# Single-bank PSUM tiles, folds on VectorE, natural query order and a pinned instruction order in a fused attention and gate kernel

## The chip, the cores and the metric

The kernel runs on one core of a Trainium2 chip. The metric is the device time of one execution in microseconds, and its median is quoted. The core has a matrix engine (PE, with its weight loads as PEld), VectorE (DVE), ScalarE (ACT), GpSimd (POOL) and SyncE (SP), which run side by side and wait for one another through semaphores. PE writes its results to a memory called PSUM; the changed program divides what it uses of it into eight tiles of 2 KB a partition, here called banks. DVE and ACT read them there; no instruction of POOL does in these kernels. The profile is of one execution; its span is about 2 us shorter than that execution's time.

Executions of the kernel before fell between 545 and 551 us or between 552 and 556 us. A run counts as slow when it is over 1.5% above the fastest of its set. The set of the main result has two runs of the kernel before, both of the longer kind, so both count as fast. The profile of the kernel before is of a 545.95 us execution.

## The reference

```python
# b, h = 8, 8   s = 576   d = 64   f = 128
def phi(x):                                   # x: [b, h, s, d]
    proj = x @ w_phi                          # d -> f
    proj = proj - max(abs(proj), axis=-1)     # per row
    return concat([exp(proj), exp(-proj)])    # 2 f features
q_p, k_p = phi(q), phi(k)
kv  = einsum('bhsf,bhsd->bhfd', k_p, v)
z   = k_p.sum(axis=2)
x   = (q_p @ kv) / (q_p @ z + 1e-6)           # attention, heads joined: [8, 576, 512]

x1, x2, x3 = split(x @ w_proj, 3)             # 512 -> 3 x 512
x2_conv = irfft(rfft(x2, axis=1) * rfft(filter, axis=0))
out = (x1 * x2_conv * x3) @ w_out
```

The symbol `@` is a matrix product. The kernel does the attention in 16 units (half the heads of a batch each) and the gate in 8, one a batch. The Fourier transforms are matmuls with sine tables. A *fold* makes the sums and differences of rows n and 576 - n in front of the forward transform.

## The kernel before

Every piece of work is a `Step` with a nominal time for each engine. A planner orders the steps from three streams: loads, then attention, then gate as filler where attention would make the PE wait. A scheduler may still move instructions, taking emission order as priority.

```python
def proj(c, shape, name):                     # double-bank tiles, two of them
    return c.psum.tile(shape, FP32, name=name, tag="proj", bufs=2)
def b1(c, shape, dtype, name):                # single-bank tiles, four
    return c.psum.tile(shape, dtype, name=name, tag="b1", bufs=4)
...
def fold(c, eng, x, GG, k0, nk, name):
    ...
    xs = x[:, k0:k0 + nk, 0:289]
    xr = x[:, k0:k0 + nk, 576:287:-1]         # read backwards
    eng.tensor_tensor(out=eo[:, :, 0, :], in0=xs, in1=xr, op=ALU.add)
    eng.tensor_tensor(out=eo[:, :, 1, :], in0=xs, in1=xr, op=ALU.subtract)
    ...                                       # two more on eo, and a small copy
...
def main(dst, src, g0, g1):                   # loads of k, q, v: partition p takes
    nc.gpsimd.dma_start(                      # rows 4p..4p+3
        out=dst[:, g0:g1].rearrange("p g h c d -> p (g h) (c d)"),
        in_=src[b, 4 * g0:4 * g1, 0:512, :].rearrange("h (p c) d -> p h (c d)", c=4))
...
def pq_a(hp):
    pp = proj(c, [P, 2, 4, P], "Pq")
    for j in range(2):
        ...                                   # two matmuls, q^T x w_phi
    for j in range(2):                        # row order restored by a strided write
        nc.scalar.activation(s.Eqp[hp][:, j].rearrange("f (p c) -> f c p", c=4),
                             pp[:, j], AF.Exp, bias=0.0, scale=1.0)
def pq_b(hp):                                 # adds -2 max, then the same with scale=-1.0
    ...
def fld():
    fold(c, nc.gpsimd, xTs[b], c.G[b % 2], kt, 2, "x")
...
for st in pl.run([loads, attn, gate], (1, 26, 12).__getitem__):
    st.fn()
```

Here `Eqp` and `Eqm` are the positive and negative exponentials of the query projection `Pq`; `Ekp` and `Ekm` are those of the key projection `Pk`.

## Time and profile before

| before | |
|---|---|
| time | 554.18 us, median of 2 (552.48 to 555.89) |
| profiled span, granted PE clock | 544.2 us, 0.918 |
| PE, DVE, ACT, POOL busy | 399.0, 307.6, 346.1, 262.8 us |
| both exponentials of Pq | 128 of 1374 and 1356 ns |
| a gate with nothing beside it | 25.7 us |

The busy table and the slices of the page of the kernel before; in the slices each digit is the busy share in tenths of a fortieth of the span, and PEclk is the clock granted to the PE:

```profile
## 1 busy us (share of the span) xinstructions
PE 399.0 (73%) x3680; PEld 247.1 (45%) x3725; DVE 307.6 (57%) x575; ACT 346.1 (64%) x604; POOL 262.8 (48%) x352
...
PE   2346673767778276775666786888689899999996
...
DVE  6991493338658332952653773777356556554453
ACT  3999634897995278568659749783984460515150
POOL 9749999198327932841592151553153343400000
PEclk9996695779898877989978999999899999999999
```

No engine is full, and the PE's digits rise to 9 only at the end. The stage windows show the two regimes; columns are the window, its length, busy us with instruction counts of PE, PEld, DVE, ACT and POOL, then clock, DMA share and GB/s:

```profile
core 0: us, PE busy (x) PEld busy (x) DVE busy (x) ACT busy (x) POOL busy (x), PEclk, DMA share, GB/s
...
200.00:240.00 40.00, 28.89 (x332) 19.84 (x334) 23.41 (x43) 26.83 (x47) 23.32 (x33) 0.87 0.40 46
...
440.00:480.00 40.00, 39.69 (x271) 20.19 (x276) 25.17 (x39) 15.92 (x30) 18.36 (x18) 1.00 0.11 34
```

From 200 to 240 us the PE is busy 28.9 of 40 us beside attention; from 440 it is busy 39.7 with gates and, until 455 us, the last transposes of attention (the last folds run on POOL), while ACT and DVE have room. A gate then takes 25.7 us (like ACT copies at 485.4 and 511.1 us in the timeline). What the first regime waits for is in the chain of work that ended last, first its shares of the whole span:

```profile
PE 32%; ACT 32%; POOL 19%; issue 6%; DVE 5%; DMA 4%; POOLq 0%; DVEq 0%; ACTq 0%
```

Then a stretch of the same chain, in the order of time (start, us, what):

```profile
207.68 2.45 ACT Eqp L696 x2
...
210.80 0.87 ACT Eqm L708
211.85 1.40 ACT Eqp L696
213.25 1.14 ACT Eqm L708
214.38 1.13 ACT Eqp L696
...
216.39 1.20 ACT Eqm L708
```

The groups of instructions (engine, operation, out<-in, count; busy us, mean ns; idle before and its releaser) give the price of those exponentials and, for comparison, that of Pk:

```profile
L708 ACT ACTIVATE Eqm<-Pq 128x512 bf16<-128x512 f32 x64 | 85.1, 1356 | 9.4 <-PE Pq L705 8.7 <-PE KV L724 0.5
L696 ACT ACTIVATE Eqp<-Pq 128x512 bf16<-128x512 f32 x64 | 81.2, 1374 | 41.2 <-PE Pq L690 41.0
...
L601 ACT ACTIVATE Ekp<-Pk 128x512 bf16<-128x512 f32 x64 | 40.3, 629 | 27.0 <-DVE mxk L598 26.9
```

Both read 128x512 fp32 and write 128x512 bf16. The only difference is the output's step, 8 bytes against 2, and the time doubles.

### The profile page before, as it was taken

To read this page: it belongs to the slowest core of one execution; us is meant where nothing else is said; L and a number is where in the kernel's file an instruction comes from. 1 tells how busy PE (TensorE), PEld (TensorE's weight loads), DVE (VectorE), ACT (ScalarE), POOL (GpSimd) and SP (SyncE) were. 2 spreads that over 40 slices of the span, in tenths; PEclk is the share of its full clock that TensorE was granted. 3 is DMA by queue.
4 is the path that set the end of the run, shared out by engine and by line. 5 is a ranking of instruction groups with operands and counts; after the bars stand their busy time and mean duration, and the time that the engine had idled before them with its cause. 6 is when DMAs were issued, how large, how long until landed. Compare 5 with 4: busy or idle time off the path is not lost.

```text
span 544.2 us, 9323 instructions
## 1 busy us (share of the span) xinstructions
PE 399.0 (73%) x3680; PEld 247.1 (45%) x3725; DVE 307.6 (57%) x575; ACT 346.1 (64%) x604; POOL 262.8 (48%) x352
## 2 busy tenths in 40 slices
PE   2346673767778276775666786888689899999996
PEld 2234562444445253553443464545445545454443
DVE  6991493338658332952653773777356556554453
ACT  3999634897995278568659749783984460515150
POOL 9749999198327932841592151553153343400000
PEclk9996695779898877989978999999899999999999
DMA  6993494047009103704533000200020020211202
GB/s 69 150 201 44 46 130 45 12 52 81 2 2 124 7 3 38 90 16 87 77 43 43 0 2 13 75 1 2 1 88 0 3 87 1 89 46 42 78 12 87
DMA packets 45707, 27.04 MB, mean 50 GB/s; under 512 B 14752, under 2 KB 40544, under 8 KB 45664
## 3 DMA queue, kind: packets, MB, share of 16 engines
q0 software_dynamic: 40256, 16.88, 26.0%
q1 hardware_dynamic: 5408, 9.57, 5.2%
q8 instruction: 29, 0.48, 0.3%
q14 instruction: 14, 0.11, 0.1%
HBM read 33.75 MB, written 9.44 MB: 79 GB/s over the span
## 4 chain that ended last, share of the span: by engine, by line
PE 32%; ACT 32%; POOL 19%; issue 6%; DVE 5%; DMA 4%; POOLq 0%; DVEq 0%; ACTq 0%
ACT Eqp L696 12%; ACT Eqm L708 11%; PE acc L928 9%; PE acc L969 6%; PE acc L893 3%; DMA ks<-in_k_dram 3%; PE acc L995 3%; ACT Ekp L601 2%; ACT Ekm L602 2%; PE Pq L705 2%; PE NE L744 2%; ACT CS L903 1%; POOL eox L365 1%; DVE mxk L598 1%; DMA out_dram<-o 1%
## 5 line engine op out<-in xcount | busy, mean ns | idle before, releaser
L696 ACT ACTIVATE Eqp<-Pq 128x512 bf16<-128x512 f32 x64 | 81.2, 1374 | 41.2 <-PE Pq L690 41.0
L708 ACT ACTIVATE Eqm<-Pq 128x512 bf16<-128x512 f32 x64 | 85.1, 1356 | 9.4 <-PE Pq L705 8.7
L928 PE MATMUL acc<-xT,wproj 128*128 128x64 bf16 (+1 forms) x501 | 66.6, 286 | 1.1 <-ACT x1s L938 0.5
L705 PE MATMUL Pq<-mT,sel 128*128 128x512 bf16 x64 | 28.4, 443 | 50.6 <-ACT Eqp L696 33.6
L598 DVE TENSOR_REDUCE mxk<-Pk 128x4 f32<-128x512 f32 x64 | 43.7, 685 | 30.5 <-PE Pk L589 26.4
L601 ACT ACTIVATE Ekp<-Pk 128x512 bf16<-128x512 f32 x64 | 40.3, 629 | 27.0 <-DVE mxk L598 26.9
L895 ACT CAST x2n<-acc 128x512 bf16<-128x512 f32 x40 | 24.1, 617 | 44.4 <-PE acc L893 21.3
L928 PEld LDWEIGHTS <-wproj 128*128 128x128 bf16 x512 | 34.0, 98 | 35.2 <-issue 6.3
L969 PE MATMUL acc<-IV,Y 128*128 128x512 bf16 (+1 forms) x255 | 40.0, 292 | 0.5
L602 ACT ACTIVATE Ekm<-Pk 128x512 bf16<-128x512 f32 x64 | 39.2, 613 | 0.0
L589 PE MATMUL Pk<-wpp,kT 128*128 128x256 bf16 x128 | 22.9, 312 | 13.2 <-DVE mxq_244 L624 6.1
L1001 DVE COPY o<-acc 128x512 f32<-128x512 f32 (+1 forms) x24 | 16.5, 687 | 28.2 <-PE acc L995 19.5
L728 ACT CAST KVs<-KV 128x260 bf16<-128x260 f32 x32 | 14.1, 443 | 28.8 <-PE KV L724 28.8
L748 DVE RECIPROCAL rc<-NE 128x10 f32<-128x10 f32 x32 | 6.9, 218 | 44.2 <-PE NE L744 44.1
L721 PEld LDWEIGHTS <-Ekp 128*128 128x128 bf16 x256 | 16.1, 106 | 31.7 <-issue 24.3
L744 PE MATMUL NE<-KVs,Eqp 128*128 128x65 bf16 x256 | 24.7, 199 | 7.5 <-ACT Eqm L708 6.7
L624 DVE TENSOR_REDUCE mxq_251<-Qn 128x8 f32<-128x1024 f32 x16 | 19.5, 1221 | 18.7 <-PE Qn L621 18.0
L621 PE MATMUL Qn<-wpp,qT 128*128 128x256 bf16 x128 | 21.4, 296 | 11.6 <-ACT Ekm L602 5.0
L953 DVE TENSOR_TENSOR ts<-acc,x1s 128x512 bf16<-128x512 f32 x32 | 21.9, 690 | 10.6 <-PE acc L928 10.4
L749 DVE TENSOR_TENSOR xn<-NE,rc 128x640 bf16<-128x640 f32 x32 | 26.2, 821 | 0.8
L969 PEld LDWEIGHTS <-Y 128*128 128x128 bf16 x256 | 18.9, 101 | 16.3 <-issue 2.0
L744 PEld LDWEIGHTS <-Eqm 128*128 128x128 bf16 x256 | 19.9, 101 | 13.4 <-issue 11.5
(468 smaller groups left out, 1179.7 us busy)
## 6 DMA issues: line engine op xcount, KB each, us to landing
out_dram<-o SPq DMA_DIRECT2D x32, 256.0 KB, 2.0
ks<-in_k_dram POOLq DMA_DIRECT2D x7, 512.0 KB, 6.1
qs<-in_q_dram POOLq DMA_DIRECT2D x7, 512.0 KB, 8.0
vs<-in_v_dram POOLq DMA_DIRECT2D x7, 512.0 KB, 6.0
wproj<-in_moe_w_proj_dram POOLq DMA_DIRECT2D x4, 384.0 KB, 11.3
out_dram<-o SPq DMA_DIRECT2D x8, 128.0 KB, 2.3
ks<-in_k_dram POOLq DMA_DIRECT2D x2, 256.0 KB, 4.4
qs<-in_q_dram POOLq DMA_DIRECT2D x2, 256.0 KB, 4.5
```

What stands on the lines that cost most here:

```text
L589: nc.tensor.matmul(pp[:, j, 2 * cp:2 * cp + 2, :], lhsT=s.kT[:, hp + 2 * j, cp, :], rhs=c.wpp, start=True, stop=True)
L598: nc.vector.tensor_reduce(out=mx[:, 4 * i:4 * i + 4], in_=pp[:, i], axis=AX.X, op=ALU.max, apply_absolute_value=True)
L601: nc.scalar.activation(Ep[:, j], pp[:, j], AF.Exp, bias=0.0, scale=1.0)
L602: nc.scalar.activation(Em[:, j], pp[:, j], AF.Exp, bias=0.0, scale=-1.0)
L696: nc.scalar.activation(s.Eqp[hp][:, j].rearrange("f (p c) -> f c p", c=4), pp[:, j], AF.Exp, bias=0.0, scale=1.0)
L705: nc.tensor.matmul(pp[:, j], lhsT=c.sel[:, 2 * hp + j, :], rhs=s.mT[:, 0:512], start=False, stop=True, skip_group_check=True)
L708: nc.scalar.activation(s.Eqm[hp][:, j].rearrange("f (p c) -> f c p", c=4), pp[:, j], AF.Exp, bias=0.0, scale=-1.0)
L744: nc.tensor.matmul(av[:, j, ci, :], lhsT=E, rhs=s.KVs[hp][:, j, sg, :], start=(sg == 0), stop=(sg == 1))
L749: nc.vector.tensor_tensor(out=s.xn[:, :, hp, :, :], in0=av[:, :, :, 0:HD].rearrange("p j c d -> p c j d"), in1=rc.rearrange("p j c o -> p ...
L895: nc.scalar.copy(x2n[:, m, :], acc)
L928: nc.tensor.matmul(acc, lhsT=c.wproj[:, kt, base + m * P:base + (m + 1) * P], rhs=xTs[b][:, kt, s0:s1], start=(kt == 0), stop=(kt == 3))
L969: nc.tensor.matmul(acc, lhsT=Y, rhs=c.IV[:, kt, s0:s1], start=(i == 0), stop=(i == 5))
```

## The change

Its intent: relieve ACT of the strided writes and POOL of the folds, let each PSUM bank go as soon as its own half is read, and start gates early, in an order worked out beforehand and pinned on each engine. Cut to its core (the order table, the split reductions and the smaller moves are cut):

```diff
-def proj(c, shape, name):
-    return c.psum.tile(shape, FP32, name=name, tag="proj", bufs=2)
 def b1(c, shape, dtype, name):
-    return c.psum.tile(shape, dtype, name=name, tag="b1", bufs=4)
+    return c.psum.tile(shape, dtype, name=name, tag="b1", bufs=8)
...
-            main(s.qs, q, g0, g1)
+            for ci in range(4):               # 256-byte packets in place of 1024
+                nc.gpsimd.dma_start(
+                    out=stage("qs")[:, g0:g1, :, ci].rearrange("p g h d -> p (g h) d"),
+                    in_=q[b, 4 * g0:4 * g1, ci * P:(ci + 1) * P, :].rearrange("h p d -> p h d"))
...
-            pp = proj(c, [P, 2, 4, P], "Pq")
+            pp = [b1(c, [P, 4, P], FP32, "Pq") for j in range(2)]   # also Pk, Qn, NE
-                    s.Eqp[hp][:, j].rearrange("f (p c) -> f c p", c=4), pp[:, j],
+                nc.scalar.activation(s.Eqp[hp][:, j], pp[j].rearrange("f c p -> f (c p)"),
...
-        fold(c, nc.gpsimd, xTs[b], c.G[b % 2], kt, 2, "x")          # and the filter's folds
+        fold(c, nc.vector, xTs[b], c.G[b % 2], kt, 2, "x")
...
-            if ci % 2:
-                nc.scalar.copy(o[0:rows, :], acc[0:rows, :])
-            else:
-                nc.vector.tensor_copy(o[0:rows, :], acc[0:rows, :])
+            nc.scalar.copy(o[0:rows, :], acc[0:rows, :])
...
-    for st in pl.run([loads, attn, gate], (1, 26, 12).__getitem__):
-        st.fn()
+    pl, order = make_plan(...)      # each step has a wanted time from a table; the planner takes
+                                    # the step with the least (lateness + weight * wanted time)
+    with tc.manual_schedule(engines={PE, Activation, DVE, Pool}):   # emission order is kept
+        for st in order:
+            st.fn()
```

## The prediction

> **What bounds the kernel now.** The profiled span is 544.2 us and no engine is full: PE 73%, ACT 64%, DVE 57%, POOL 48% (busy table). To about 440 us attention and gate overlap, PE busy 22 to 36 of every 40 us (stage windows). After that only gate work is left: PE busy 39.5 of 40, 25.7 us a batch (like ACT copies at 485.4 and 511.1 us in the timeline). Before that the chain of waits runs through ACT: the exponentials of Pq are 22% of the span (all ACT 32%), POOL 19%; PE waits 33.6 and 16.4 us for those exponentials (waits). They cost 1374 and 1356 ns; those of Pk, of the same shape and types, 629 and 613. Only the output step differs (8 bytes against 2); the trace agrees with the Trainium skill, "SBUF — State Buffer", the note on cachelines: full rate needs at least two hits in a 16-byte line.
>
> **What changes.**
> - Natural q order makes those 128 writes contiguous: about -95 us of ACT. 24 output copies come from DVE: +15. ACT 346 -> 266 us.
> - Folds leave POOL: 16 x about 5.3 us and two filter folds, -99 us. q loads become four DMAs each: 27 more issues at 0.9 us. POOL 263 -> 185.
> - Folds on DVE: 18 of four tensor_tensors and small copies. Contiguous bf16 ones of 1024 and 512 elements take 0.69 and 0.42 us here, so 0.45 for 578 in that mode, 0.75 outside it. The Trainium skill, "Vector Engine (DVE) Microarchitecture Reference", section 5.1, leaves a negative step unmeasured; one input of each reads backwards. I expect 2.2 to 3.3 us a fold: +50. Output copies -16.5, split reductions +5, split normalisation +11, memsets +3. DVE 308 -> 360: the fullest engine.
> - Eight single banks replace two double and four single slots: a bank is free after its own half.
> - The fixed order spreads the gate: the first starts once four attention units have begun, the last attention transpose is at 81% of the matmuls' time (changed instruction order).
>
> **Sum.** PE work is unchanged: 752,640 moving columns, of which a gate has 59,392; at the tail's 25.7 us per gate that is 326 us at full clock (estimate), 350 at a granted 0.93. DVE needs 360. Per batch: PE 44, DVE 41, ACT 30 us. Overlap will not be perfect: I take 48 to 49 us a batch, 388 for eight, plus 35 us of start (sine tables, DVE 35 busy of the first 40 us, unchanged) and 5 of drain. Predicted: 428 us, range 398 to 468, 8 in 10. About 90 of the 126 us are ACT time on the chain; the rest is the merged tail and POOL. Chances: faster by over 2% 0.96, within 2% 0.02, slower 0.02.
>
> **What would show it.** Right: exponentials of Pq near 0.62 us; PE busy above 7 tenths in nearly every slice after the first three; a chain of PE and DVE, almost no POOL; DVE above 80%; clock up from 0.918. Wrong: exponentials above 1 us; fold operations above 0.8 us or stretched beside POOL (before, the gate's products stretched from 0.69 to 1.68 us); a new wait for q loads, whose packets shrink from 1024 to 256 bytes.
>
> **What would make it wrong.** A fixed order from nominal times stalls all engines where real times differ (exponential 0.48 nominal, 0.6 here): then 460 or more. Folds at 0.45 us an operation: 400 or less.

## The result

The changed kernel takes 435.79 us (434.49 and 437.09) against 554.18. The ratio of the fast runs is 0.7864, 95% interval 0.7719 to 0.8008. A ratio here is the mean time of one kernel's fast runs over that of the other's of the same rounds, so it is not quite the ratio of the quoted medians. The forecast was 428, in a range of 398 to 468. The two runs of the kernel before in this set are of the longer kind; against its fast runs in the sets below (means 548 to 550 us) the gain is about 113 us and not 118, a ratio of about 0.79.

The same parts of the page, after:

```profile
## 1 busy us (share of the span) xinstructions
PE 363.8 (84%) x3725; PEld 230.3 (53%) x3725; DVE 339.9 (78%) x758; ACT 272.9 (63%) x628; POOL 183.2 (42%) x236
...
PE   1311778669997999888999988999999999999995
...
DVE  5994679965995899649999799989998889552741
ACT  1886736089665874568748965399647887354322
POOL 9964805670186326626473294329431241000000
PEclk9999988699998999999999998999999999999999
```

From the tenth slice on the digits of the PE are 9 or 8 but for one 7 and the last; its first four are lower than before. The windows that answer to those shown, and the first:

```profile
core 0: us, PE busy (x) PEld busy (x) DVE busy (x) ACT busy (x) POOL busy (x), PEclk, DMA share, GB/s
0.00:40.00 40.00, 7.71 (x46) 5.29 (x46) 28.61 (x86) 26.16 (x44) 30.31 (x50) 1.00 1.04 129
...
200.00:240.00 40.00, 37.22 (x439) 24.79 (x438) 38.83 (x84) 27.87 (x70) 23.40 (x28) 1.00 0.58 73
...
360.00:400.00 40.00, 39.11 (x337) 20.97 (x335) 23.87 (x50) 21.15 (x41) 0.32 (x1) 1.00 0.09 31
```

From 200 to 240 us the PE does gate and attention together, 37.2 us busy, and DVE is busy 38.8 of 40. The chain has gone over to these two, over the whole span:

```profile
DVE 43%; PE 37%; ACT 9%; POOL 4%; issue 3%; DMA 3%; ACTq 0%; POOLq 0%
```

and in the same stretch as before, from about 200 us:

```profile
211.32 1.20 DVE mxk L595 x2
212.51 1.79 DVE ts L946 x3
214.31 1.20 DVE mxq_247 L621 x2
...
216.68 1.28 DVE mxq_247 L621 x2
217.95 1.19 DVE mxk L595 x2
...
220.77 0.60 DVE yT_262 L972
```

The groups, in the order of those above, and the first two operations of a fold, now on DVE:

```profile
L598 ACT ACTIVATE Ekp<-Pk 128x512 bf16<-128x512 f32 x64 | 39.2, 612 | 59.7 <-PE Pk L586 41.3 <-DVE mxk L595 18.1
...
L704 ACT ACTIVATE Eqm<-Pq 128x512 bf16<-128x512 f32 x64 | 36.3, 663 | 3.1 <-PE Pq L699 3.1
L691 ACT ACTIVATE Eqp<-Pq 128x512 bf16<-128x512 f32 x64 | 34.9, 629 | 1.2 <-PE Pq L685 1.1
...
L363 DVE TENSOR_TENSOR eox<-xT 128x578 bf16<-128x578 bf16 x16 | 9.8, 610 | 0.6
...
L364 DVE TENSOR_TENSOR eox<-xT 128x578 bf16<-128x578 bf16 x16 | 7.7, 479 | 0.0
```

The exponentials of Pq now cost what those of Pk cost.

### The profile page after: what moved, and what is told of

The parts are those of the page before. It is cut to its first block, busy times and chain, and to the rows that moved or that the text cites. A ratio compares the mean times of both kernels' runs of the same rounds, so it can differ in the third digit from the quotient of the medians.

```text
span 435.2 us, 9441 instructions
## 1 busy us (share of the span) xinstructions
PE 363.8 (84%) x3725; PEld 230.3 (53%) x3725; DVE 339.9 (78%) x758; ACT 272.9 (63%) x628; POOL 183.2 (42%) x236
## 4 chain that ended last, share of the span: by engine, by line
DVE 43%; PE 37%; ACT 9%; POOL 4%; issue 3%; DMA 3%; ACTq 0%; POOLq 0%
PE acc L962 5%; DVE mxk L595 5%; PE acc L921 5%; PE acc L886 5%; PE acc L988 5%; DVE xn L743 4%; DMA out_dram<-o 3%; DVE mxq_247 L621 3%; DVE ts L946 3%; DVE mxq_254 L621 2%; PE KV L716 2%; DVE xT L766 2%; PE Pq L685 2%; PE NE L738 2%; PE Pq L699 1%
## 5 line engine op out<-in xcount | busy, mean ns | idle before, releaser
L921 PE MATMUL acc<-xT,wproj 128*128 128x512 bf16 (+1 forms) x512 | 72.5, 288 | 0.0
L962 PE MATMUL acc<-IV,Y 128*128 128x512 bf16 (+1 forms) x256 | 38.9, 286 | 0.0
L704 ACT ACTIVATE Eqm<-Pq 128x512 bf16<-128x512 f32 x64 | 36.3, 663 | 3.1 <-PE Pq L699 3.1
L991 ACT COPY o<-acc 128x512 f32<-128x512 f32 (+1 forms) x40 | 23.5, 601 | 21.0 <-PE acc L988 12.5
L691 ACT ACTIVATE Eqp<-Pq 128x512 bf16<-128x512 f32 x64 | 34.9, 629 | 1.2 <-PE Pq L685 1.1
L511 POOL DMA_DIRECT2D qs<-in_q_dram x36 | 31.3, 906 | 5.0 <-DMA wproj<-in_moe_w_proj_dram 3.9
L743 DVE TENSOR_TENSOR xn<-NE,rc 128x320 bf16<-128x320 f32 x64 | 31.4, 491 | 2.2
L896 ACT CAST CS<-acc 128x512 bf16<-128x512 f32 x40 | 23.1, 622 | 13.7 <-PE acc L378 11.1
L738 PE MATMUL NE<-KVs,Eqm 128*128 128x65 bf16 x256 | 22.7, 196 | 0.0
L738 PEld LDWEIGHTS <-Eqp 128*128 128x128 bf16 x256 | 19.6, 99 | 3.0 <-DVE kT L562 0.4
L621 DVE TENSOR_REDUCE mxq_254<-Qn 128x4 f32<-128x512 f32 x32 | 20.0, 682 | 0.7 <-PE Qn L618 0.6
```

The lines of the kernel that those rows point to most:

```text
L511: nc.gpsimd.dma_start(out=stage("qs")[:, g0:g1, :, ci].rearrange("p g h d -> p (g h) d"), in_=q[b, 4 * g0:4 * g1, ci * P:(ci + 1) * P, :]. ...
L621: nc.vector.tensor_reduce(out=mxq[:, 0:4, 2 * hp + j], in_=pp, axis=AX.X, op=ALU.max, apply_absolute_value=True)
L691: nc.scalar.activation(s.Eqp[hp][:, j], pp[j].rearrange("f c p -> f (c p)"), AF.Exp, bias=0.0, scale=1.0)
L704: nc.scalar.activation(s.Eqm[hp][:, j], pp[j].rearrange("f c p -> f (c p)"), AF.Exp, bias=0.0, scale=-1.0)
L738: nc.tensor.matmul(av[:, ci, :], lhsT=E, rhs=s.KVs[hp][:, j, sg, :], start=(sg == 0), stop=(sg == 1))
L743: nc.vector.tensor_tensor(out=s.xn[:, :, hp, j, :], in0=av[:, :, 0:HD], in1=rc.to_broadcast([P, 5, HD]), op=ALU.mult)
```

## The experiments

Each kernel was run four times (three rounds and a profile) beside the kernel before, whose median over all its runs, slow ones included, lay between 553.6 and 554.8 us in every set. The ratios use its fast runs (mean 548 to 550 us), and so do the gains given here. The sets ran on different chips, so a difference of a few us between kernels of different sets is uncertain. All gave correct results. The changed kernel itself was not run again in these sets, so it enters with its 435.8 us from its own set. "Pinned" is the fixed order on every engine.

### e1: natural query order alone, in the kernel before

```diff
-            main(s.qs, q, g0, g1)
+            (the four DMAs of the change)
-                    s.Eqp[hp][:, j].rearrange("f (p c) -> f c p", c=4), pp[:, j],
+                    s.Eqp[hp][:, j], pp[:, j].rearrange("f c p -> f (c p)"),     # Eqm alike
```

> The kernel before with one part of the change: natural q order (four q DMAs a load, contiguous exponentials of Pq). Theory A (the ACT time on the chain is most of the gain): exponentials of Pq fall to about 0.62 us, ACT busy from 346 to about 255 us, time about 490 us (0.88 of before); the gate-only tail of about 100 us stays, which is why it is not 440. Rival B (the merged order is the gain, ACT was only one of several equal chains): 530 us or more, the chain moving to POOL.

Measured: 501.28 us (500.54 to 502.65), ratio 0.9118 (0.9044 to 0.9192). ACT fell to 264.5 us busy and the exponentials to 616 and 621 ns, about as forecast. The gain is 49 us against the fast runs, from 82 us less ACT work. ACT falls from 32% of the chain to 10%, and the shares are now these:

```profile
PE 44%; POOL 25%; DVE 10%; ACT 10%; issue 6%; DMA 5%; POOLq 0%; DVEq 0%; ACTq 0%
```

The windows at the end of the same profile:

```profile
core 0: us, PE busy (x) PEld busy (x) DVE busy (x) ACT busy (x) POOL busy (x), PEclk, DMA share, GB/s
400.00:440.00 40.00, 40.00 (x277) 20.15 (x276) 26.80 (x41) 13.61 (x26) 15.74 (x16) 1.00 0.09 31
440.00:480.00 40.00, 40.00 (x257) 19.42 (x255) 19.21 (x33) 16.55 (x31) 0.00 (x0) 1.00 0.18 60
```

POOL is now a quarter of the chain (19% before), and at the end there are again 80 us and more in which the PE is full, DVE is a third to a half idle and ACT more than half. Theory A comes nearer (about 490 forecast); rival B's 530 was missed, but it is right that other chains stood close behind ACT.

### e2: the strided writes put back into the changed kernel

```diff
-            (the four DMAs of the change)
+            main(stage("qs"), q, g0, g1)
-                nc.scalar.activation(s.Eqp[hp][:, j], pp[j].rearrange("f c p -> f (c p)"),
+                nc.scalar.activation(s.Eqp[hp][:, j].rearrange("f (p c) -> f c p", c=4), pp[j],   # Eqm alike
```

> The changed kernel with one part undone: q loaded and exponentials written in the old order (8-byte output step), everything else and the instruction order kept. Theory A: ACT busy rises by 90 us to about 365, ACT becomes the fullest engine, time about 475 us (1.09 of the changed kernel). Rival B: ACT had 37% idle, the order hides most of it, below 450 us.

Measured: 495.95 us (495.49 to 496.07), ratio to before 0.9017 (0.8946 to 0.9088), 60 us more than the changed kernel. ACT is busy 354.2 us and is 38% of the chain. It is the fullest engine after the PE, but with 72% not a full one; the loss is larger than either theory said. It may be that in the pinned order every late exponential also delays what stands behind it; that is argued, not shown.

### e3: the folds back on POOL

```diff
-        fold(c, nc.vector, xTs[b], c.G[b % 2], kt, 2, "x")
+        fold(c, nc.gpsimd, xTs[b], c.G[b % 2], kt, 2, "x")     # and the filter's, and the border copy
```

> The changed kernel with the folds back on POOL, order kept. Theory A: DVE drops by 40 us to about 300, POOL rises to about 283 us; a fold takes 5.3 us in place of 2.3 and v products wait behind it, time 455 to 470 us, POOL on the chain again. Rival B: DVE was the fullest engine (37 to 39 of 40 us busy between 200 and 320 us), so its relief wins and the time is 430 us or less.

Measured: 449.45 us (449.40 to 450.00), ratio 0.8173 (0.8094 to 0.8251), 14 us slower than the changed kernel. POOL rose to 286.4 us busy and is 12% of the chain. DVE fell to 310.4, by 29.5 us and not by the 50 that the folds had taken: part of it went into the gate's products on DVE, whose groups rose from 32.4 to 40.9 and from 11.1 to 16.6 us. The trace shows them slowed beside the folds on POOL: of the 48 products of 1024 elements in those groups, the 18 with no POOL instruction beside them took 0.68 to 0.69 us, and all 12 that took 1.17 to 1.77 us ran beside a fold operation. The folds' move is worth 14 us although it loads the engine that is now the fullest after the PE: nearer to theory A, but below its 455 to 470 us.

### e8: the order rule of before, pinned

```diff
-        (make_plan's table)
+        return pl, pl.run_streams([loads, attn, gate], (1, 26, 12).__getitem__)
```

> The changed kernel with the order rule of the kernel before (three streams, attention first, gate filling in), still fixed on each engine; all else of the change kept. Theory A: a gate-only tail of about 100 us comes back, in which DVE and ACT are under half busy, and their work is squeezed into the rest: 465 to 480 us. Rival B: the order is worth little once ACT is relieved: below 445 us.

Measured: 478.18 us (475.09 to 481.31), ratio 0.8696 (0.8612 to 0.8779), 42 us slower than the changed kernel. The windows from 360 us show the gates alone again:

```profile
core 0: us, PE busy (x) PEld busy (x) DVE busy (x) ACT busy (x) POOL busy (x), PEclk, DMA share, GB/s
360.00:400.00 40.00, 40.00 (x373) 22.57 (x372) 25.63 (x62) 15.79 (x30) 0.00 (x0) 1.00 0.12 43
400.00:440.00 40.00, 40.00 (x263) 19.50 (x262) 20.71 (x39) 19.49 (x36) 0.00 (x0) 1.00 0.14 48
```

PE full, DVE 20.7 to 25.6 and ACT 15.8 to 19.5 of 40. In the changed kernel DVE's work is spread, and only the last 75 us look like that. This is theory A. The Trainium skill ("Perfetto Trace Analysis", Optimization Strategy) says that where the most-contended engine changes over time, interleaving those regimes may help; here it is worth 42 us.

### e4 and e5: the pinning alone

```diff
-    with tc.manual_schedule(engines={...}):
-        for st in order:
-            st.fn()
+    for st in order:                       # e4: the changed kernel, free
+        st.fn()
```

e5 does the reverse: the loop of the kernel before is put into `manual_schedule`.

> The changed kernel without the fixed order per engine: the instructions are emitted in the same order, but the scheduler may move them. Theory A (what counts is the merged emission order, the pinning little): 437 to 450 us. Rival B (the pinning itself carries the order's 42 us): 470 us or more.

> The kernel before, with its own emission order pinned on each engine, nothing else. Theory A: pinning alone is worth little, ratio 0.97 to 1.03 (538 to 570 us). Rival B: pinning is a good part of the gain, below 525 us.

Measured: e4 420.56 us (419.79 to 421.72), ratio 0.7681 (0.7637 to 0.7724); e5 640.18 us (638.07 to 641.18), ratio 1.1684 (1.1613 to 1.1754). Both misses: pinning is not worth little, it costs. It costs 92 us in the kernel before (against its fast runs) and 15 us in the changed one. e4 is the fastest kernel. Of DVE's waits this one changes most (us in total, times, longest us), here pinned:

```profile
DVE mxk L595 <- ACT Ekm L599: 17.0, 13, 5.7
```

and here free:

```profile
DVE mxk L595 <- ACT Ekm L599: 5.4, 8, 2.4
```

The maxima of Pk, kept in their place, stand 17.0 us behind exponentials of ACT; free, 5.4 us. That these waits make up the 15 us is not shown. DVE leads the chain no more: PE 53%, DVE 33%, in place of DVE 43% and PE 37%. The order of emission still counts when it isn't pinned, as e10 shows.

### e13: only the PE pinned

```diff
-    with tc.manual_schedule(engines={PE, Activation, DVE, Pool}):
+    with tc.manual_schedule(engines={PE}):
```

> The changed kernel with only the PE pinned to the planned order; ACT, DVE and POOL are left to the scheduler. It asks where the 15 us between the changed kernel (436) and the unpinned one (421) lie. Theory A (the planned order of DVE and ACT, made from durations that are too short for them, is what stalls; the PE order is good): 419 to 426 us. Rival B (the PE order holds up the others): 432 to 438 us.

Measured: 425.85 us (425.35 to 426.05); no ratio was given, as only one of the seven runs of the kernel before in this set counted as fast (545.91 us; the others 554.45 to 555.44). Of the 15 us, about 10 come back when DVE, ACT and POOL are free, and about 5 lie in the PE's order (about 1%, between different sets, so uncertain). Theory A, with a share for the PE. That the short nominal times are the reason fits the numbers (0.48 us nominal for a 512-element exponential, 0.61 to 0.66 measured; 0.60 for a 512-element reduction, 0.68 measured), but no plan with corrected times was run, so the reason was only argued.

### e6 and e9: double-bank tiles, pinned and free

```diff
-    return c.psum.tile(shape, dtype, name=name, tag="b1", bufs=8)
+    return c.psum.tile(shape, dtype, name=name, tag="b1", bufs=4)
+def pair2(c, name):
+    t = c.psum.tile([P, 2, 4, P], FP32, name=name, tag="proj", bufs=2)
+    return [t[:, 0], t[:, 1]]
-            pp = [b1(c, [P, 4, P], FP32, "Pq") for j in range(2)]
+            pp = pair2(c, "Pq")                                   # Pk, Qn and NE alike
```

> The changed kernel with the memory of before for matmul results: two double-bank tiles for Pk, Qn, Pq and the normaliser, four single-bank ones for the rest; the order, made for eight single banks, is kept. Theory A: a pair is free only when both halves are read, so the matmuls in front of DVE reductions and ACT exponentials wait longer: 450 to 470 us, new waits of Pk, Qn and NE matmuls for DVE and ACT. Rival B: banks were never short, 440 us or less.

> The changed kernel with two double-bank and four single-bank tiles (as e6) and without the pinned order (as e4). Theory A (most of the 154 us of e6 are an order made for eight banks that cannot move; the banks themselves are worth less): 440 to 470 us, 20 to 50 over the 421 of e4. Rival B (single banks are the largest part of the change whatever the order): 520 us or more. Rival C (worth nothing): within 8 us of e4.

Measured: e6 589.50 us (586.18 to 592.45), ratio 1.0762 (1.0673 to 1.0850), slower than the kernel before. e9 464.0 to 465.2 us in its three fast runs, ratio 0.8462 (0.8358 to 0.8566). e6 is 154 us over the changed kernel, far past theory A; e9 is 44 us over e4, as its theory A said. So the single banks are worth some 44 us, and another 110 us of e6 is an order that was made for eight banks and could not move. The order of emission of e9 was still the one made for eight banks, so part of the 44 us may be the order's; that was not tested. The new waits of the PE in e6, longest first (us in total, times, longest us):

```profile
PE NE L746 <- DVE xn L751: 49.0, 32, 3.4
PE Qn L624 <- DVE mxq L627: 33.1, 32, 5.3
```

In the changed kernel neither wait is among the PE's ten longest.

One execution of e9, the profiled one, took 965.72 us and is left out. It is described in the last section.

### e10: the order rule of before, free

> The changed kernel with the order rule of before (as e8) and without pinning (as e4). Theory A (the merged order of emission is worth its 42 us also to a scheduler that may move things, since it works by emission order): 455 to 475 us. Rival B (the scheduler recovers the merging by itself): 430 us or less.

Its edit is that of e8 and that of e4 together. Measured: 452.87 us (449.87 to 454.84), ratio 0.8239 (0.8116 to 0.8362). That is 32 us over e4 and 25 under e8. The result lies between the theories and close to A: the merged order is worth 32 us even to a scheduler that may move instructions.

### e7: output copies back on DVE

```diff
-            nc.scalar.copy(o[0:rows, :], acc[0:rows, :])
+            (nc.vector.tensor_copy for even ci, as before)
```

> The changed kernel with 24 of the 40 output copies back on DVE: DVE plus 16 us (about 356), ACT minus 15. Theory A (DVE is nearly full from 200 to 320 us, so it is the limit there): 5 to 12 us slower, 441 to 448 us. Rival B (PE and waits limit it): within 3 us of the changed kernel.

Measured: 439.70 us (438.65 to 440.17), ratio 0.8022 (0.7968 to 0.8076). DVE's busy time rose by 13.6 us and the time by 4 us, a little under theory A. The difference is about 1%, between kernels of different sets, so the size is uncertain.

### e12: an attempt at something faster

The six tables of the inverse transform are made just before the first gate needs them, in tiles of their own, without pinning.

```diff
-    for g in trig_groups(c):
+    trig = trig_groups(c)
+    for g in trig[:4]:
         g()
...
     for st in order:
+        if st.name == "m0.x10":
+            for g in trig[4:]:             # POOL writes the counter again for each
+                g()
         st.fn()
```

> An attempt at something faster: e4 with the six sine tables of the inverse transform made just before gate 0 needs them and not in the first 40 us (their DVE work of about 10 us and their table loads leave the start; an integer counter is written by POOL each time). Theory A (DVE work is the chain of the first 60 us): 8 to 12 us off e4, 408 to 413 us. Rival B (the same work is only moved to where DVE is nearly full as well): 418 us or more.

Measured: 431.33 us (431.28 to 433.27), ratio 0.7864 (0.7786 to 0.7943), 11 us slower than e4. A failure, as rival B expected. The start did get faster: the PE was busy 19.0 of the first 40 us, against 13.5 in e4. The loss came where the tables went (65.7 to 121.0 us in the trace): from 100 to 120 us the PE was busy 12.3 of 20 us, against 19.4 in e4. Its new waits are for the products of v on POOL (7.4 us), which the counters may have delayed; that was not tested.

## Why the prediction was right

The time was 8 us above the forecast and well inside the range. Point by point:

- **Strided writes: right in mechanism, too large on the chain.** 1374 and 1356 ns became 629 and 663. ACT was forecast at 266 us and measured 272.9. But "about 90 of the 126 us are ACT time on the chain" was too much: natural order alone gave 49 us (e1), and its removal from the changed kernel cost 60 (e2). The other terms are larger than "the rest".
- **Merged regimes: right, and larger than I made it.** 42 us pinned (e8), 32 us free (e10).
- **Single banks: not sized in the prediction.** 44 us when the instructions may move (e9). They are not a detail.
- **Folds: right in size, with one of its own signs of error in part.** Each of the four operations was expected at 0.45 to 0.75 us and measured a mean of 0.48 to 0.61; but 11 of the 72 were stretched to between 0.65 and 1.32 us beside products on POOL. The groups of the folds sum to 43 us of DVE, with the small copies at the borders 50 (50 forecast). POOL was forecast at 185 us and measured 183.2. The net worth was 14 us (e3).
- **DVE: 360 us forecast, 339.9 measured.** The busy times of DVE's groups sum to about 333 us before and 376 after, a rise of 43 against the 52 forecast: the split reductions cost 1 us (38.9 to 40.0), not 5, and the memsets 1.5, not 3. The other 11 us are overlap. The sum over groups counts operations of different groups that overlap twice; the engine's busy time counts them once, and it rose by 32. Two reductions of 0.68 us stand in the chain with 1.20 us.
- **PE work: right in the sum by luck.** The forecast counted 752,640 columns; the trace of the changed kernel has 785,152, which at the same rate are 340 us and not 326. But the granted clock was 0.975 and not 0.93, and 340 at 0.975 gives 348 (an estimate), close to the 350 forecast. The PE's busy time is 363.8 us.
- **The sum: a start that was too small, over half of it made up by the rest.** "35 us of start" is the step that was mis-sized. The first window shows the PE busy 7.7 us, against 13.6 before. Counting matmul columns at the tail's rate of 25.7 us per 59,392 (an estimate from the traces), about 23 of the 340 us of PE work were done by 80 us. The other 317 us, 7.5 of 8 batches, took the remaining 355 us: about 47.6 us a batch, with the drain in it, against the forecast 48 to 49 without. Eight batches at that rate are 381 us, which leaves about 55 us for the start. So the start took 20 us more than forecast, and batches and drain 12 less (381 against 388 + 5). Pinning is a small part of it: unpinned (e4), about 25 us of PE work were done by 80 us, 2 to 3 us more.
- **What would show it.** Confirmed: a chain of DVE 43% and PE 37%, POOL 4%; clock 0.918 to 0.975; the PE's digit at 7 or more in every slice from the tenth to the last but one. Not confirmed: the slices from the fourth to the ninth (two of them at 6, one at 1), and DVE above 80% (78%). Of the signs of error, a new wait for q loads showed only once (the PE for `qt`, 3.9 us).
- **The fixed order.** I named it as a danger and did not price it. It costs 15 us (e4). The 4 parts undone one at a time cost 60, 42, 14 and 44 (the last measured without pinning), which is more than the 113 to 118 us gained: the parts help one another, and their worths do not add up. The split reductions and normalisation and the smaller moves were not undone alone.

## What to carry to other kernels

Spreading a stage that needs only one engine over the stage that needs the others was worth 32 to 42 us here, and it needs the order of emission, not pinned engines: with the same order left to the scheduler the kernel ran in 421 us in place of 436. An order made for one number of buffers is worth little with another: with the old tiles the pinned plan ran in 590 us, the free one in 465. Where one operation costs twice its like, look at the step of its output first.

## What the Trainium skill lacked or had wrong

- "Vector Engine (DVE) Microarchitecture Reference", section 5.1, lists an operand with a negative step as not measured. Here a bf16 addition of 578 elements a partition with one input read backwards took a median of 468 ns and the subtraction 454. Forward ones of 512 and 1024 elements took about 0.42 and 0.69 us, so 578 should take some 0.45 (an estimate from those two). The backward step is as fast as the forward one.
- "SBUF — State Buffer", in the note on cachelines, says that full rate needs at least two hits in a 16-byte line. A step of 8 bytes puts two elements in each line, so by the note it should cost nothing. Here a bf16 output of ScalarE with a step of 8 bytes took 1374 ns where the contiguous one took 629, a factor of 2.2. The same page's "Who interferes with whom" says that a DVE operation with two inputs in SBUF contends with a POOL operation that reads SBUF, and gives no factor that fits a fold. The trace agrees: of the 72 operations of the folds, the 11 that took 652 to 1315 ns all ran beside one of POOL's products of v, and the other 61 took 448 to 471 ns.
- "TensorE: Matmul & The Clock Gate", in the caveats under "Seeing it yourself", tells of a PE clock held far down for 50 us and more, and of records not to be trusted. One execution of e9 looks like that for its whole 964 us. That the clock was the cause is an inference: weight loads (a median of 101 ns against 98) and ACT's activations (592 against 597) were as in the changed kernel, and only matmuls were slow. One of its windows, with columns as above (the clock is third from the end):

```profile
500.00:600.00 100.00, 97.42 (x414) 50.28 (x419) 37.24 (x76) 29.79 (x68) 21.47 (x27) 1.00 0.24 30
```

And one of its groups of matmuls:

```profile
L996 PE MATMUL acc<-wout,yT 128*128 128x512 bf16 x153 | 99.9, 835 | 2.6 <-issue 2.6
```

  The record gives full clock, and 128x512 matmuls take 835 ns where those of the changed kernel's same line take 379. The other three took 465 us.
- No page weighs a pinned order against a scheduler's. Pinning cost 15 us of 436 in the changed kernel, and 92 us on top of 548 in the kernel before.
